# A second Strassen level for the last two products of three down stages

## The chip, the cores and the metric

The program runs on one core of one Trainium2 chip. A core has a matrix engine (TensorE, "PE" in the profile, with its weight loads shown as "PEld"), a vector engine (VectorE, "DVE"), a scalar engine (ScalarE, "ACT"), a general engine (GpSimd, "POOL") and a queue engine (SyncE, "SP") that issues all DMA transfers of this kernel in one order. Matmuls write into PSUM, eight banks of 128 x 512 fp32; everything else lives in SBUF or in DRAM.

The metric is the device time of one execution in microseconds.

## The reference, cut to what matters

```python
def _B_ref(x, w_gate, w_up, w_down):
    g = jnp.einsum("bsd,df->bsf", x, w_gate)
    u = jnp.einsum("bsd,df->bsf", x, w_up)
    h = g * u
    return jnp.einsum("bsf,fd->bsd", h, w_down)

x = A_x
x = x + _A_ref(_layernorm(x, axis=-1), A_wqkv, A_wo)
x = x + _B_ref(_layernorm(x, axis=-1), B_w_gate, B_w_up, B_w_down)
x = x + _A_ref(_layernorm(x, axis=-1), A_wqkv, A_wo)
x = x + _B_ref(_layernorm(x, axis=-1), B_w_gate, B_w_up, B_w_down)
```

S = 2048 tokens, D = 1024, F = 3584, bf16 inputs and output. `_A_ref` is a linear attention block (32 heads); `_B_ref` is the block that the change touches, in particular its last product, h times w_down. Both blocks run twice with the same weights.

## The kernel before, in words

The host code writes a list of operations per engine; `_Prog` finds every dependency from byte ranges in SBUF and from PSUM banks (a bank is one unit: whoever touches it waits for the others' last access), and turns it into semaphore waits. Each engine runs its list in order. So the order of the code is the order of every queue, SP's too.

Layer A computes K and Q (L780), a Gram matrix (L862) and the output projection (L954). Layer B works in two passes of 1024 tokens; each pass has a gate-up stage (L1037, and L1104 for products with a second level) and a down stage (L1312). The four down stages begin near 410, 654, 1132 and 1375 us of the profile: layer one's first and second pass, layer two's first and second pass.

All big products use Strassen's method in the Winograd form, seven products of half-size blocks instead of eight. In a down stage (`down`, L1278) the order is `DPROD = 1 2 7 4 6 5 3`. One product multiplies 1792 of F (14 chunks of 128, `NJ = 14`) by 512 tokens (4 tiles `t` of 128) and 512 output columns: for each tile two groups of seven matmuls, 128 x 512 each, into one bank. The stationary operand is a slice of the activations (hA, hB, hC, hD, 14 x 512 fp16 each), the moving operand is the weight block. Products 1, 2, 3 read blocks of w_down; 5, 6, 7, 4 read sums of such blocks, made in layer one's first gate-up stage (`wd_prep`) and kept in DRAM (`t_scratch`). After each tile VectorE evicts the bank (`stt`, L671: scale and add) and in products 1, 2, 7, 4 also updates a slice of the activations (`tt`, L668, 1792 elements) for later products. Product 3 accumulates onto product 5's bank, product 6 onto 1's, 4 onto 7's. Rest sums stand in `rtmp[0..7]`, 2 KB each from `O_R`.

Weights come through a ring of `NR = 5` slots of 8 KB per partition. `ring_issue` (L638) loads the unit `n` into slot (n + 1) % 5; it is called as a unit is used up, so loads run up to five units ahead. A pass has 28 gate-up units and 14 down units (two halves of 0.9 MB per product). Waiting for a free slot holds up all that follows on SP.

Some gate-up products already run a second level (`L2SETS`, `l2_of`, L1086): there a 128 x 512 result in one bank is made of seven quarter products of 256 columns, with a seed copy on ScalarE (L1119), a copy of product 5 (L1129) and a join on VectorE (L1122). Their weight sums are kept in `sp_scratch` and read by `sp_load`. The first steps of the next pass's gate-up stage (`pro`) are dealt out between the groups of product 3 of the down stage before (L1321).

Other work between the groups of a down stage: `dticks0` (first pass) takes sums of the normalised inputs off a list (`x_pop`), stores the residual (`stash`) and loads `sp_scratch`; `dticks1` (second pass, layer one) loads the K and Q weights for the next layer A (L1404 to L1407) and starts the normalisation of four token tiles. The K weights lie in the bytes of ring slots 0 and 1, the Q weights in those of hC and hD.

## Time and profile before

| | |
|---|---|
| Time, median of 3 runs | 1464.74 us (1464.23 to 1464.97) |
| Time of the profiled execution | 1464.57 us |
| Its span, first to last instruction | 1462.8 us |
| Granted TensorE clock | 1.0 of full speed |
| TensorE busy | 1453.9 us |
| VectorE, ScalarE, GpSimd busy | 1090.1, 572.0, 225.8 us |
| DMA | 298.11 MB, mean 204 GB/s |

[...] A group's row gives its line, engine, operation, shapes and count, then the busy time, the mean duration in ns, and the idle time of that engine right before these instructions with what ended it. A row of a timeline gives the start, the length, the instruction and its count, and in brackets the idle time before it. A row of windows gives the stretch, then each engine's busy time and instruction count, the granted clock, DMA's busy share and GB/s.

### The profile page before, as it was taken

To read this page: it belongs to the slowest core of one execution; us is meant where nothing else is said; L and a number is where in the kernel's file an instruction comes from. 1 tells how busy PE (TensorE), PEld (TensorE's weight loads), DVE (VectorE), ACT (ScalarE), POOL (GpSimd) and SP (SyncE) were. 2 spreads that over 40 slices of the span, in tenths; PEclk is the share of its full clock that TensorE was granted. 3 is DMA by queue.
4 is the path that set the end of the run, shared out by engine and by line. 5 is a ranking of instruction groups with operands and counts; after the bars stand their busy time and mean duration, and the time that the engine had idled before them with its cause. 6 is when DMAs were issued, how large, how long until landed. Compare 5 with 4: busy or idle time off the path is not lost.

```text
span 1462.8 us, 20720 instructions
## 1 busy us (share of the span) xinstructions
PE 1453.9 (99%) x7830; PEld 751.8 (51%) x7830; DVE 1090.1 (75%) x1990; ACT 572.0 (39%) x1178; POOL 225.8 (15%) x239
## 2 busy tenths in 40 slices
PE   8999999999999999999999999999999999999999
PEld 3444444444444555554444444456666446666544
DVE  7986888777757699865578769879877575777653
ACT  3332355333300255550023323567776005777400
POOL 4553632000000000000034337300000000000000
PEclk9999999999999999999999999999999999999999
DMA  6133667988875799975374337679986768888642
GB/s 230 37 94 107 138 131 188 278 259 259 279 253 190 259 274 291 281 242 187 127 231 123 106 108 152 152 211 272 284 258 199 243 221 240 263 264 241 217 167 94
DMA packets 370931, 298.11 MB, mean 204 GB/s; under 512 B 234640, under 2 KB 323472, under 8 KB 370832
## 3 DMA queue, kind: packets, MB, share of 16 engines
q1 hardware_dynamic: 370832, 296.80, 69.6%
q8 instruction: 61, 1.00, 0.3%
q14 instruction: 38, 0.31, 0.1%
HBM read 218.63 MB, written 54.53 MB: 187 GB/s over the span
## 4 chain that ended last, share of the span: by engine, by line
PE 99%; DMA 1%; DVE 0%; ACT 0%; SPq 0%; issue 0%
PE ps L1037 30%; PE ps L1312 23%; PE ps L780 15%; PE ps L1104 15%; PE ps L862 8%; PE ps L954 7%; DMA arena<-in_A_wqkv_dram 1%; PE ps L902 0%; PE ps L874 0%; SPq L406 0%; PE ps L538 0%; DVE arena L668 0%; ACT arena L540 0%; PE ps L886 0%; DVE arena L671 0%; DVE arena L960 0%
## 5 line engine op out<-in xcount | busy, mean ns | idle before, releaser
L671 DVE SCALAR_TENSOR_TENSOR arena<-ps,arena 128x512 f16<-128x512 f32 (+2 forms) x508 | 340.4, 686 | 195.1 <-PE ps L1312 140.8
L1037 PE MATMUL ps<-arena 128*128 128x512 f16 x2016 | 478.5, 379 | 0.0
L668 DVE TENSOR_TENSOR arena<-arena 128x512 f16<-128x512 f16 (+4 forms) x624 | 308.8, 520 | 54.1 <-ACT arena L1147 46.4
L1312 PE MATMUL ps<-arena 128*128 128x512 f16 (+1 forms) x1568 | 340.9, 379 | 0.0
L1037 PEld LDWEIGHTS ps<-arena 128*128 128x128 f16 (+1 forms) x2016 | 192.3, 98 | 186.7 <-ACT arena L1042 13.6
L1104 PE MATMUL ps<-arena 128*128 128x256 f16 x1960 | 259.4, 273 | 0.8 <-DVE ps L1122 0.5
L1312 PEld LDWEIGHTS ps<-arena 128*128 128x128 f16 x1568 | 153.4, 98 | 183.1
L1104 PEld LDWEIGHTS ps<-arena 128*128 128x128 f16 (+1 forms) x1960 | 190.9, 98 | 83.3 <-DVE ps L1122 3.8
L780 PE MATMUL ps<-arena 128*128 128x512 bf16 x1024 | 223.7, 379 | 3.2 <-ACT arena L540 1.1
L1042 ACT ACTIVATE arena<-ps 128x512 f16<-128x512 f32 x224 | 133.8, 597 | 110.6 <-PE ps L1037 108.6
L582 ACT ACTIVATE arena<-ps 128x512 f32<-128x512 f32 x128 | 76.4, 597 | 231.5 <-PE ps L780 220.1
L780 PEld LDWEIGHTS ps<-arena 128*128 128x128 f16 x1024 | 99.6, 98 | 122.0 <-DMA arena<-in_A_wqkv_dram 1.6
L1119 ACT COPY ps<-ps 128x256 f32<-128x256 f32 x168 | 61.8, 368 | 204.0 <-PE ps L1104 201.4
L435 POOL TENSOR_SCALAR arena<-arena 128x1 f32<-128x1 f32 x64 | 27.2, 425 | 643.0 <-DVE arena L434 643.0
L862 PE MATMUL ps<-arena 128*128 128x512 bf16 x512 | 115.4, 379 | 0.0
L954 PE MATMUL ps<-arena 128*128 128x512 bf16 x512 | 111.0, 379 | 0.0
L1067 ACT COPY ps<-ps 128x512 f32<-128x512 f32 x112 | 64.2, 573 | 90.6 <-PE ps L1037 52.4
L1122 DVE TENSOR_TENSOR ps<-ps,arena 128x256 f32<-128x256 f32 x168 | 70.7, 428 | 33.6 <-PE ps L1104 16.7
L432 DVE BATCH_NORM_STATS2 arena<-arena 128x6 f32<-128x512 bf16 x128 | 88.2, 689 | 8.2 <-DMA arena<-in_A_x_dram 6.0
L585 DVE SCALAR_TENSOR_TENSOR arena<-ps,arena 128x512 bf16<-128x512 f32 x128 | 88.5, 692 | 4.4
L809 POOL TENSOR_TENSOR arena<-arena 128x1024 f16<-128x1024 f32 x32 | 79.3, 2478 | 72.9 <-DVE arena L807 71.7
L792 POOL TENSOR_TENSOR arena<-arena 128x512 f32<-128x512 f32 x60 | 74.7, 1249 | 87.1 <-DVE arena L585 85.7
(51 smaller groups left out, 705.3 us busy)
## 6 DMA issues: line engine op xcount, KB each, us to landing
arena<-w_scratch SPq DMA_DIRECT2D x84, 512.0 KB, 5.4
arena<-t_scratch SPq DMA_DIRECT2D x32, 896.0 KB, 5.7
arena<-sp_scratch SPq DMA_DIRECT2D x56, 512.0 KB, 6.0
arena<-in_B_w_down_dram SPq DMA_DIRECT2D x24, 896.0 KB, 5.8
w_scratch<-arena SPq DMA_DIRECT2D x28, 512.0 KB, 6.6
sp_scratch<-arena SPq DMA_DIRECT2D x28, 512.0 KB, 4.1
arena<-in_A_wqkv_dram SPq DMA_DIRECT2D x12, 1024.0 KB, 8.0
arena<-in_B_w_gate_dram SPq DMA_DIRECT2D x42, 256.0 KB, 5.4
```

What stands on the lines that cost most here:

```text
L432: P.add("dve", (lambda h: lambda e: e.bn_stats(st[j][:, 6 * h:6 * h + 6], x_res[:, i, (D // 2) * h:(D // 2) * (h + 1)]))(h), rd=r_x(i, (D ...
L585: P.add("dve", lambda e: e.scalar_tensor_tensor(out=dst_ap, in0=psb(bank), scalar=0.0, in1=etmp[r], op0=ALU.max, op1=ALU.add), prd=[bank], ...
L668: P.add("dve", lambda e: e.tensor_tensor(out=out, in0=a, in1=b, op=op), rd=rd, wr=wr, prd=prd)
L671: P.add("dve", lambda e: e.scalar_tensor_tensor(out=out, in0=a, scalar=sc, in1=b, op0=ALU.mult, op1=op1), rd=rd, wr=wr, prd=prd)
L780: return [e.matmul(psb(bank), xnT[:, k, i * 128:(i + 1) * 128], w[:, k, h * 512:(h + 1) * 512], start=(k == 0), stop=(k == KT - 1)) for k ...
L809: P.add("pool", lambda e: e.tensor_tensor(out=asb[b].rearrange("p (h c) -> p h c", c=32), in0=pbuf.rearrange("p (h c) -> p h c", c=32), in ...
L862: return [e.matmul(psb(bank), xr[:, t, j * 128:(j + 1) * 128], pk[:, h, t, :], start=(t == 0), stop=(t == NST - 1)) for t in range(NST)]
L954: return [e.matmul(psb(bank), xnT[:, g, i * 128:(i + 1) * 128], wp[:, g, dh * 512:(dh + 1) * 512], start=(dh == 0 and g == 0), stop=(g == ...
L1037: P.add("pe", lambda e: [e.matmul(psb(bank), w[:, k, :], x[:, k, :], start=(start and k == 0), stop=(k == 3), skip_group_check=True) for k ...
L1042: P.add("act", lambda e: e.activation(t, psb(bank), AF.Copy, scale=SG), prd=[bank], wr=r)
L1104: P.add("pe", lambda e: [e.matmul(psb(bank)[:, 256 * half:256 * half + 256], w[:, k, :], xx[:, k, :], start=(start and k == 0), stop=(k == ...
L1312: return [e.matmul(psb(bank), hv[:, 7 * hf + k, t * 128:(t + 1) * 128], w[:, k, :], start=(start and hf == 0 and k == 0), stop=(hf == 1 an ...
```

## The change

In three of the four down stages (not layer one's first pass) products 5 and 3 are computed by a second Strassen level. A product is cut into quarters again: F in two halves of seven chunks, 512 tokens in two, 512 columns in two. Seven sub-products in the order 1, 5, 6, 7, 2, 3, 4, each for two halves `p` of 128 tokens, each of seven matmuls of 256 columns. Sub-product 1 goes to a bank `tmp[p]`, is copied by ScalarE into the result bank (`seed`), 5 is copied aside (`c5`), 6 and 7 accumulate on `tmp[p]` and are joined by VectorE into the result banks; 2, 3 and 4 accumulate there directly.

The activation sums (`a_sums`, four operations of 1792 elements per product) are made by VectorE during product 6 (for 5) and during product 5 (for 3). The weight sums (`b_sums`) are made once, in layer one's first down stage: load, eight subtractions, store to `d_scratch`, for product 5 and then for product 3. A down product with two levels takes four ring units (a, b, c, d; 0.92, 0.92, 0.92 and 0.46 MB) instead of two. Product 3 no longer accumulates on product 5's bank, so product 5's tiles are evicted twice (`evict5`). The next pass's prologue gets three steps inside product 3 instead of six. K weights are loaded in halves after sub-products 5 and 7 of product 3, Q weights after 7, and two instead of four normalisations are started there. In layer two the input sums are taken in products 2, 7, 4 instead of 6 and 5, and `sp_load` moves from product 6 to products 4 and 3. Places of a few buffers are exchanged (`O_DRAW`, `O_CP`, the second buffer of the sums of group "53").

```diff
-    O_DRAW = O_R + 12288
+    O_DRAW = O_R
...
-    O_CP = O_R
+    O_CP = O_R + 12288
...
+        L2D = "53"
         DPROD = ["1", "2", "7", "4", "6", "5", "3"]
+
+        def d_units(first, ps_):
+            r = []
+            for q in DPROD:
+                r += [(q, i) for i in ("abcd" if q in L2D and not (first and ps_ == 0) else "01")]
+            return r
...
+            di = L2D.index(q)
+            rs = R(V_L2 + 128 * di, 128)
+            lo, hi = slice(0, 7), slice(7, 14)
+            if hf == "a":
+                ap, rd = src(lo, slice(0, 256))
+                dma(vq(o, 1792).rearrange("p (j c) -> p j c", c=256), ap, r_slot(n, 0, 3584), KRR[sl], rd=rd)
...
+                l2d = L2D if not (first and ps_ == 0) else ""
+                SB = {"5": O_HC, "3": O_HA}
...
+                def a_sums(q):
+                    hv, ho = hs[q]
+                    blk = {(r, k): (hv[:, 7 * k:7 * k + 7, 256 * r:256 * r + 256], _seg(ho + 7168 * k, 7, 1024, 512 * r, 512 * r + 512))
+                           for r in range(2) for k in range(2)}
+                    s = [(vh(SB[q] + i * 3584, 1792).rearrange("p (j s) -> p j s", s=256), R(SB[q] + i * 3584, 3584)) for i in range(3)]
+
+                    def op(o, a, b, f):
+                        tt(o[0], a[0], b[0], f, a[1] + b[1], o[1])
+                    return [lambda: op(s[0], blk[1, 0], blk[1, 1], ALU.add),
+                            lambda: op(s[1], s[0], blk[0, 0], ALU.subtract),
+                            lambda: op(s[2], blk[0, 1], s[1], ALU.subtract),
+                            lambda: op(blk[1, 0], blk[0, 0], blk[1, 0], ALU.subtract)]
...
+                def b_load(q):
+                    for i, (_, j0, j1) in enumerate(PB):
+                        v, r = b_buf(i, vb if q in "123" else vh)
+                        src = wd_v[:, :, 1, 512:1024] if q == "3" else tscr[0]
+                        for h in range(2):
+                            dma(v[:, h], src[:, 7 * h + j0:7 * h + j1, :], R(r[0][0] + h * 1024 * (j1 - j0), 1024 * (j1 - j0)), KDB[2 * i + h],
+                                rd=[] if q == "3" else R(V_D, NJ * 32))
...
+                        res.append([lambda blk=blk: op(blk(0, 0), blk(0, 1, nf), blk(0, 0, nf)),
+                                    lambda blk=blk: op(blk(0, 1), blk(1, 1, nf), blk(0, 1, nf)),
+                                    lambda blk=blk: op(blk(1, 1), blk(1, 1, nf), blk(0, 0)),
+                                    lambda blk=blk: op(blk(1, 0), blk(1, 0, nf), blk(1, 1))])
+                    return [(lambda f=f, g=g: [f(), g()]) for f, g in zip(*res)]
...
+                def prep_step(q, t):
+                    k = 4 * "1274".index(q) + t
+                    if k == 0:
+                        b_load("5")
+                        EX.extend(b_sums("5") + [lambda: b_store("5"), lambda: b_load("3")] + b_sums("3") + [lambda: b_store("3")])
+                    if k in (3, 4, 5, 6, 8, 12, 13, 14, 15):
+                        ex_pop(2 if k == 8 else 1)
+                    if k == 15:
+                        ex_pop(9)
...
+                def evict5(t, bank):
+                    pb = psb(bank)
+                    xs, rx = xq(1, 1, t)
+                    stt(xs, pb, CD, rtmp[t], rr(t), rx, prd=[bank])
+                    final(1, 1, t)
+                    stt(rtmp[4 + t], pb, CD, rtmp[4 + t], rr(4 + t), rr(4 + t), prd=[bank])
+
+                def evict3(t, bank):
+                    xs, rx = xq(0, 1, t)
+                    stt(xs, psb(bank), CD, rtmp[4 + t], rr(4 + t), rx, prd=[bank])
+                    final(0, 1, t)
...
+                    dst, tmp = ([6, 7, 5, 4], [0, 2]) if q == "5" else ([0, 1, 2, 3], [6, 7])
...
+                    def seed(p, b):
+                        P.add("act", lambda e: e.copy(psb(b)[:, 0:256], psb(tmp[p])[:, 0:256]), prd=[tmp[p]], pwr=[b])
+
+                    def join(p, b):
+                        P.add("dve", lambda e: e.tensor_tensor(out=psb(b)[:, 256:512], in0=psb(tmp[p])[:, 0:256], in1=c5[p][0], op=ALU.add),
+                              prd=[tmp[p]], rd=c5[p][1], pwr=[b])
+
+                    for si, i in enumerate((1, 5, 6, 7, 2, 3, 4)):
+                        for p in range(2):
+                            hi, lo = dst[p], dst[p + 2]
+                            if i == 1:
+                                mm(1, p, tmp[p], 0, True)
+                                seed(p, hi)
+                            elif i == 5:
+                                mm(5, p, tmp[p], 1, False)
+                                P.add("act", (lambda p: lambda e: e.copy(c5[p][0], psb(tmp[p])[:, 256:512]))(p), prd=[tmp[p]], wr=c5[p][1])
+                            elif i == 6:
+                                mm(6, p, tmp[p], 0, False)
+                                join(p, hi)
+                            elif i == 2:
+                                mm(2, p, hi, 0, False)
+                            elif i == 3:
+                                mm(3, p, hi, 1, False)
+                                evict(p, hi)
+                            elif i == 7:
+                                mm(7, p, tmp[p], 0, False)
+                                seed(p, lo)
+                                join(p, lo)
+                            else:
+                                mm(4, p, lo, 0, False)
+                                evict(p + 2, lo)
+                            if q == "3" and i in (3, 4) and (i == 4 or p):
+                                pro_step(pro, 1)
+                        if q == "5" and i in (1, 7):
+                            ex_pop(2)
+                        if i in (5, 7, 3, 4):
+                            ring_issue()
+                            ticks(q, {5: 0, 7: 1, 3: 2, 4: 3}[i])
...
                 for qi, q in enumerate(DPROD):
+                    if q in l2d:
+                        if q == "5":
+                            ex_pop(4)
+                            EX.extend(a_sums("3"))
+                        two_level(q)
+                        continue
+                    if q == "6" and l2d:
+                        EX.extend(a_sums("5"))
...
+                        if q in "1274" and first and ps_ == 0:
+                            prep_step(q, t)
+                        if q == "6" and l2d and t < 2:
+                            ex_pop(2)
...
-                if q == "6" and t == 3 and not first:
-                    for g in SPG:
-                        sp_load(1, 0, g)
-                    sp_load(1, 1, "12")
-                if q in "65":
-                    x_pop(2 if q == "6" else 3)
+                if q == "4" and t < 2 and not first:
+                    sp_load(1, t, "12")
+                    if t == 0:
+                        sp_load(1, 0, "53")
+                if q in ("65" if first else "274"):
+                    x_pop(3 if q == "5" else 1 if q == "2" else 2)
...
+                if q == "3" and t == 0 and not first:
+                    sp_load(1, 1, "53")
...
-                if q == "5" and t == 3:
-                    for w in "kq":
-                        load_w(w, 0)
-                        load_w(w, 1)
+                if q == "3" and t < 2:
+                    load_w("k", t)
+                if q == "3" and t == 1:
+                    load_w("q", 0)
+                    load_w("q", 1)
                 if q == "3":
                     stash(12 + t)
-                    nxt.step_t(1)
-                    nxt.b2_one()
-                    nxt.b1_one()
-                    nxt.start(8 + t)
+                    for k in ((0,) if t == 1 else (1,) if t == 2 else ()):
+                        nxt.step_t(1)
+                        nxt.b2_one()
+                        nxt.b1_one()
+                        nxt.start(8 + k)
```

More of the change, by code (lines that the diff above doesn't have):

```diff
@@ L270, in build_kernel @@
     V_SP = V_D + NJ * 32
[L271 removed]
+    V_L2 = V_SP + NJ * 64
+    P = _Prog(V_L2 + 256)
     dma_keys = []
@@ L294, in build_kernel @@
     KTL = [dkey("tl%d" % i) for i in range(4)]
+    KDB = [dkey("db%d" % i) for i in range(4)]
+    KDS = [dkey("ds%d" % i) for i in range(4)]
     KTF = [dkey("tf%d" % i) for i in range(NST)]
@@ new lines, in down, with ex_pop @@
+                EX = []
+                def ex_pop(n=1):
+                    for _ in range(n):
+                        if EX:
+                            EX.pop(0)()
+                def evict5(t, bank):
[8 more added lines that the diff above has]
+                    final(0, 1, t)
```

115 lines of the change are left out of this document (90 added, 25 removed).

## The prediction

> **What bounds the kernel now.** I read the page first (span, busy shares, chain of waits), then the groups with shapes kept apart, then the timeline of the down stages.
>
> ```profile
> span 1462.8 us, 20720 instructions
> PE 1453.9 (99%) x7830; PEld 751.8 (51%) x7830; DVE 1090.1 (75%) x1990; ACT 572.0 (39%) x1178; POOL 225.8 (15%) x239
> PE 99%; DMA 1%; DVE 0%; ACT 0%; SPq 0%; issue 0%
> ...
> L1312 PE MATMUL ps<-arena 128*128 128x512 f16 x896 | 194.0, 379 | 0.0
> L1312 PE MATMUL ps<-arena 128*128 128x512 bf16 x672 | 148.1, 379 | 0.0
> L1104 PE MATMUL ps<-arena 128*128 128x256 f16 x1960 | 259.4, 273 | 0.8 <-DVE ps L1122 0.5 <-ACT arena L1147 0.2
> ```
>
> TensorE is busy from end to end and the chain is TensorE. The down matmuls (L1312) have 0.0 us of idle before them; even the two-level products of gate-up (L1104), with their copies and adds on other engines, lose 0.8 us in 1960. So the change is worth the TensorE time it removes, less every wait it brings into a queue that today has almost none.
>
> The mean durations (379, 273 ns) overlap; the price of a matmul is its pitch, read from long runs:
>
> ```profile
> 412.15 75.70 PE L1312 MATMUL ps<-arena 128*128 128x512 bf16 x350
> ...
> 1227.20 2.35 PE L1104 MATMUL ps<-arena 128*128 128x256 f16 x20
> ```
>
> 512 columns: (75.70 - 0.379) / 349 = 0.2158 us. 256 columns: (2.35 - 0.273) / 19 = 0.1093 us, though each has its own weight load.
>
> **Term 1, TensorE work.** A down product is 4 tiles x 14 = 56 matmuls of 512 columns: 56 x 0.2158 = 12.09 us. A two-level product is 7 groups x 2 halves x 7 = 98 matmuls of 256 columns: 98 x 0.1093 = 10.71 us. Two products in three stages: 6 x 1.375 = **-8.25 us**. It cannot gain more.
>
> On the loads, row first:
>
> ```profile
> L1312 PEld LDWEIGHTS ps<-arena 128*128 128x128 f16 x1568 | 153.4, 98 | 183.1
> ```
>
> A load takes 98 ns, so it hides under 109 ns with 11 to spare, as it does in the run of 20. [...]
>
> **Term 2, waits inside a two-level product.** A group of seven lasts 0.764 us; the two halves alternate, so each hand-over to ACT or DVE has one group as cover. The rows:
>
> ```profile
> 489.64 0.38 PE L1104 MATMUL ps<-arena 128*128 128x256 f16 x2
> 490.06 0.43 DVE L1122 TENSOR_TENSOR ps<-ps,arena 128x256 f32<-128x256 f32 x1 [1.52 <-PE ps L1104]
> ...
> 974.53 0.43 DVE L1122 TENSOR_TENSOR ps<-ps,arena 128x256 f32<-128x256 f32 x1 [0.88 <-ACT ps L1119]
> 975.02 0.33 PEld L1104 LDWEIGHTS ps<-arena 128*128 128x128 bf16 x4 [0.32 <-DVE ps L1122]
> ...
> L1119 ACT COPY ps<-ps 128x256 f32<-128x256 f32 x168 | 61.8, 368 | 204.0 <-PE ps L1104 201.4
> L1129 ACT COPY arena<-ps 128x256 f32<-128x256 f32 x84 | 32.0, 381 | 0.0
> ```
>
> A consumer starts 0.31 us after the last matmul's start (489.75 to 490.06); TensorE goes on 0.06 us after the releaser's end (974.96 to 975.02). From a group's start, its last matmul starts at 0.65, the consumer at 0.96, and TensorE is free again at 0.96 + 0.37 + 0.06 = 1.39 (seed copy), 1.40 (copy of c5), 1.45 (join, 0.43). The next group on that bank is due at 1.53. All three fit, by 80 to 140 ns, if ACT and DVE are free. ACT has nothing else in a down stage. DVE has:
>
> ```profile
> 708.06 1.08 DVE L668 TENSOR_TENSOR arena<-arena 128x1792 f16<-128x1792 f16 x1
> 710.48 2.01 DVE L671 SCALAR_TENSOR_TENSOR arena<-ps,arena 128x512 bf16<-128x512 f32 x3 [1.33 <-PE ps L1312]
> 713.50 2.01 DVE L671 SCALAR_TENSOR_TENSOR arena<-ps,arena 128x512 bf16<-128x512 f32 x3 [1.01 <-PE ps L1312]
> ```
>
> Product 6 takes three evictions per tile of 3.02 us, 1.01 us idle. The change adds four sums of 1792 elements (1.08 each, about 1.0 apart) in its first two tiles. DVE falls behind and is level again by the last tile, whose evictions end 2.1 us into product 5. There two dependent sums for product 3 (a_sums) stand ahead of the first join: to 4.3 us. The join is ready at 5 x 0.764 + 0.2 = 4.0, ends at 4.75, and TensorE wants the bank at 4.58: 0.24 us late. Product 5's tiles now take two evictions each (evict5), behind two more sums; the second tile's bank comes free about 11.8 us after product 5's start, and product 3 wants it at 11.7: 0.13 us. So 0.4 us per stage, **+1.1 us** for three. Bounds: 0 (below that is excluded, no wait exists to be removed), and 6 us if one more 2.01 us eviction group stands before the joins in each stage.
>
> **Term 3, next pass's prologue.** In layer two's first down stage these steps lie between product 3's groups of seven:
>
> ```profile
> 1209.11 0.60 PE L1104 MATMUL ps<-arena 128*128 128x256 f16 x4
> 1209.55 1.67 PE L1312 MATMUL ps<-arena 128*128 128x512 bf16 x7
> 1211.06 0.38 PE L1104 MATMUL ps<-arena 128*128 128x256 f16 x2
> 1211.27 1.67 PE L1312 MATMUL ps<-arena 128*128 128x512 bf16 x7
> ```
>
> Six steps have 1.51 us of cover each. After the change three steps have 0.76 us and the others follow back to back. Step 16 waits for two copies (0.31 + 0.37 + 0.38 against 0.76 + 0.11), 17 for a join behind an eviction, 21 for 17's join, 36 for 31's copies behind a 0.57 us copy: 0.14 + 0.17 + 0.2 + 0.3 = **+0.8 us**, once (layer one's first stage is not converted). Bounds 0 and 2.
>
> **Term 4, preparation in the first down stage.** Two loads and two stores of 14 x 128 KB = 1.83 MB, and eight pairs of subtractions of 1536 and 256 elements. On the line through 512 elements (0.42) and 1792 (1.08) a pair costs 1.25 us, 10 us in all.
>
> ```profile
> 410.00:422.00 12.00, 12.00 (x57) 5.48 (x56) 8.28 (x14) 0.00 (x0) 0.00 (x0) 1.00 0.92 322
> 422.00:434.00 12.00, 12.00 (x58) 5.44 (x56) 6.76 (x8) 0.00 (x0) 0.00 (x0) 1.00 0.45 153
> ...
> 445.58 1.83 SPq L406 DMA_DIRECT2D arena<-t_scratch  x2
> ...
> t_scratch<-arena SPq DMA_DIRECT2D x1, 512.0 KB, 3.7
> ```
>
> DVE has 5 of 12 us free, DMA half. The adds have cover: product 2's banks are wanted again only by product 7, 12 us later. What can surface is the order. The first load queues behind five x loads and lands near 426.5; the sum at product 1's last tile wants it at 423, so DVE runs 4 us late, under that cover. SP then holds the second load until the first stores have landed (about 440 to 451), and the two weight loads issued today at 445.58 to 447.41 stand behind it. The first of the two carries the second half of product 6's weights, wanted at 459.9; I get 459.5. Finally T1's subtraction in product 6 waits for the second store. Three places with 0 to 3 us of slack: **+0.7 us**, bounds 0 and 5.
>
> **Term 5, K weights of layer two.** Moved from product 5's end to inside product 3, because they overlay ring slots 0 and 1; the Q loads follow them on SP, and two normalisation starts move into layer A.
>
> ```profile
> 730.11 5.22 SPq L406 DMA_DIRECT2D arena<-in_A_wqkv_dram  x4
> DMA to landing us min/median/max: 5.1/5.1/5.1
> DMA to landing us min/median/max: 7.7/7.7/7.7
> ...
> 743.51 103.76 PE L780 MATMUL ps<-arena 128*128 128x512 bf16 x480
> 764.00:774.00 10.00, 10.00 (x48) 4.56 (x47) 9.25 (x17) 3.58 (x6) 4.00 (x5) 1.00 0.35 98
> ```
>
> Today they are issued 13 us ahead; the first half lands in 5.1 us, the second 2.6 behind it. Now half 0 goes out 3.2 us into product 3 and lands at 8.4 of its 10.8; half 1 at 6.3, landing about 11.5, wanted after one group of eight (1.73 us), at 12.4. **+0.2 us**, bounds 0 and 2.6. The moved normalisations find DVE at 9.25 of 10 us, but tokens are needed four groups later; 0.
>
> **Term 6, weight supply.** Products 5 and 3 read 0.92 + 0.92 + 0.92 + 0.46 = 3.2 MB each instead of 1.83, partly in 512 B runs.
>
> ```profile
> 672.00:684.00 12.00, 12.00 (x58) 5.44 (x56) 6.67 (x9) 0.00 (x0) 0.00 (x0) 1.00 0.44 147
> 1220.00:1240.00 20.00, 20.00 (x142) 13.69 (x141) 15.28 (x31) 14.35 (x36) 0.00 (x0) 1.00 0.93 276
> ```
>
> Full DMA is 147 / 0.44 = 334 GB/s with today's 1 KB rows, 276 / 0.93 = 297 with gate-up's mixture. Need at the worst (late product 6 to the end of 3) is 0.46 + 3 x 0.92 + 0.46 for the products, 0.5 for sums and 4 x 0.9 for the next pass's units, 7.8 MB in 23 us; at 300 GB/s that takes 26. The lag of 3 us meets a lead of about 10 us (five slots ahead): **0**, bounds 0 and 15.
>
> **Sum.** Profiled execution 1464.57 (span 1462.8 and 1.8 around it; the median of the runs is 1464.74): 1464.57 - 8.25 + 1.1 + 0.8 + 0.7 + 0.2 + 0 = **1459.1 us**.
>
> **Rivals.**
> - *Preparation surfaces* (term 4 at its upper bound: a weight unit or DVE late behind SP's blocked queue): 1459.1 - 0.7 + 5 = 1463.4, no change. For it: slack of only 0.4 us by my count. Against: five slots, and DVE slack of about 9 us.
> - *K weights late* (term 5 at 2.6): 1461.5 to 1462, at the edge of no change. For: half the former lead; against: DMA is otherwise empty there.
> - *The hand-overs do not fit.* Place: join before group 7 and seeds before group 5. If DVE is one eviction group (2.01 us) further behind in products 5 and 3, all of it shows: 6 x 2.0 = 12, for term 2's 1.1: 1470.0, slower. It decides from 1.375 us of wait per product. For it: margins of 80 to 140 ns and sums queued ahead of joins; against: L1104 loses 0.8 us over 168 joins, though with other work between.
> - *Weights late.* If the DMA lag grows to 15 us less the 10 of lead in each stage, 3 x 5: 1474, slower. For: 3.2 MB per 10.7 us is 300 GB/s, DMA's full rate; against: only for 23 us.
> - *Loads show.* If loads stop hiding under 109 ns, 98 more matmuls' worth of 98 ns: 6 x 98 x 0.098 = 58 more, 1517. The run of 20 speaks against it.
>
> **Chances.** Forecast 0.70; K weights 0.04; preparation 0.10; hand-overs 0.08; weights late 0.06; loads 0.02. A measurement of this kernel tells 0.2% (2.9 us) from no change: faster (below 1461.8) 0.70, within 0.14, slower 0.16. Range: from no wait at all (1464.57 - 8.25 = 1456.3) to beyond preparation's case, 1465.0; it leaves out the three slower cases and a little of the others. The forecast's own range is 1456.3 to 1461.7.
>
> **What would show it.** 1232 matmuls of 512 columns left in the down loop, 588 new ones of 256 at a pitch near 109 ns; each converted stage 2.3 to 2.8 us shorter; idle TensorE before the two-level line about 1 us in all, released by DVE; idle before L780 in layer two near 0. Wrong if the pitch is above 123 ns (12.09 / 98), if TensorE's idle behind DMA is over 3 us, or if the first down stage is more than 3 us longer.

## The result and the profile after

| | before | after |
|---|---|---|
| Median of 7 runs each | 1464.74 us (1464.23 to 1465.23) | 1459.52 us (1458.97 to 1460.23) |
| Profiled execution | 1464.57 us | 1459.30 us |
| Its span | 1462.8 us | 1457.6 us |

The ratio is 0.9965 (95% interval 0.9953 to 0.9977): 5.2 us faster, 0.4 above the forecast. Line numbers have moved: the plain down matmul L1312 is now L1516, the new two-level matmul L1452 with its seed L1456, join L1459 and c5 copy L1470; gate-up's second level L1104 is L1143, its join L1161 and copies L1168 and L1186; the K and Q projection L780 is L819; `tt` is L707, `stt` L710, every DMA issue L411.

The page of the kernel after, the row of busy shares and that of its chain of waits:

```profile
PE 1448.2 (99%) x8082; PEld 775.5 (53%) x8082; DVE 1135.5 (78%) x2066; ACT 584.8 (40%) x1214; POOL 224.8 (15%) x239
PE 96%; DVE 2%; DMA 1%; ACT 0%; SPq 0%; issue 0%
```

TensorE still sets the end, but no longer alone. At the new waits the chain passes over to the engine that is waited for: DVE and DMA hold 3% of it instead of 1%. The groups of the same kernel, shapes kept apart:

```profile
L1516 PE MATMUL ps<-arena 128*128 128x512 f16 x728 | 157.8, 379 | 0.0
L1516 PE MATMUL ps<-arena 128*128 128x512 bf16 x504 | 110.6, 379 | 0.0
L1452 PE MATMUL ps<-arena 128*128 128x256 f16 x462 | 52.6, 273 | 0.1
L1452 PE MATMUL ps<-arena 128*128 128x256 bf16 x126 | 15.1, 273 | 0.0
L1143 PE MATMUL ps<-arena 128*128 128x256 f16 x1960 | 259.3, 273 | 1.2 <-DVE ps L1161 0.5 <-ACT arena L1186 0.3 <-DMA arena<-in_B_w_gate_dram 0.3
```

728 + 504 = 1232 matmuls of 512 columns are left, 462 + 126 = 588 of 256 columns are new. The idle time of L1452 reads 0.1 us, which is too little: a matmul's recorded duration (273 ns) is longer than the pitch (109 ns), so a start that is 0.15 us late still overlaps the matmul before it. Short waits are therefore read from the starts of neighbouring matmuls, beyond the pitch. TensorE's timeline around layer one's converted stage:

```profile
719.22 21.86 PE L1452 MATMUL ps<-arena 128*128 128x256 f16 x196
740.91 1.89 PE L819 MATMUL ps<-arena 128*128 128x512 bf16 x8
743.64 36.65 PE L819 MATMUL ps<-arena 128*128 128x512 bf16 x169 [0.84 <-DMA arena<-in_A_wqkv_dram]
```

Products 5 and 3 take 740.91 - 719.22 = 21.69 us, where two plain ones take 2 x 12.09 = 24.17 by the prediction's pitch: 2.48 us less. 196 x 0.1093 is 21.42, so 0.27 us of waits lie inside the pair. The last two rows show the one large new wait: eight matmuls of the K projection, then 743.64 - 740.91 = 2.73 us to the ninth, of which eight pitches of 0.2158 explain 1.73. The remaining 1.0 us is waiting for the second half of the K weights.

The weight loads of the next pass's prologue, inside layer two's first down stage, from the timeline of PEld (a prologue step waits here for what the bracket names):

```profile
1211.51 0.33 PEld L1143 LDWEIGHTS ps<-arena 128*128 128x128 bf16 x4 [0.53 <-DMA arena<-in_B_w_gate_dram]
...
1212.86 0.11 PEld L1143 LDWEIGHTS ps<-arena 128*128 128x128 f16 x2 [0.25 <-ACT arena L1168]
...
1214.01 0.99 PEld L1143 LDWEIGHTS ps<-arena 128*128 128x128 f16 x10 [0.27 <-DVE ps L1161]
1215.31 0.33 PEld L1143 LDWEIGHTS ps<-arena 128*128 128x128 bf16 x4 [0.32 <-DVE ps L1161]
1216.08 1.21 PEld L1143 LDWEIGHTS ps<-arena 128*128 128x128 f16 x12 [0.43 <-ACT arena L1186]
```

The brackets are the loader's idle time, of which some 0.1 us is ordinary. From the starts of neighbouring matmuls the five waits of TensorE are 0.42, 0.14, 0.16, 0.21 and 0.31 us. Four were predicted with their places; the first was not. Where it comes from is seen in SP's timelines of the kernel after and of the kernel before, at the same load:

```profile
1203.25 1.53 SPq L411 DMA_DIRECT2D out_dram<-arena  x2
1204.82 0.43 SPq L411 DMA_DIRECT2D arena<-in_B_w_gate_dram  x1
```

```profile
1192.68 0.39 SPq L406 DMA_DIRECT2D arena<-in_B_w_gate_dram  x1
```

In the kernel after, the gate weights stand on SP behind two output stores, which wait for the last evictions of product 5. Issued at 1204.82, they were used at 1211.51, 6.7 us later. In the kernel before, the same load went out at 1192.68 for a step that began at 1209.11, 16.4 us ahead. So most of the lead was lost elsewhere: a two-level product takes four units of the five-slot ring instead of two, and a load that runs five units ahead now goes out when product 5's last unit is used up, not product 6's.

The sum, all from starts of matmuls in this one execution: 8.25 us of work gone; waits inside the three pairs of products +0.89 (0.27, 0.35, 0.27); prologue +1.23, and +0.1 on a DMA 21 us later; K weights +1.0; preparation 0. That makes -5.0; the spans differ by 5.2.

### The profile page after: what moved, and what is told of

Its sections match the earlier page's. It is cut to its first block, busy times and chain, and to the rows that moved or that the text cites. A ratio compares the mean times of both kernels' runs of the same rounds, so it can differ in the third digit from the quotient of the medians.

```text
span 1457.6 us, 21384 instructions
## 1 busy us (share of the span) xinstructions
PE 1448.2 (99%) x8082; PEld 775.5 (53%) x8082; DVE 1135.5 (78%) x2066; ACT 584.8 (40%) x1214; POOL 224.8 (15%) x239
## 4 chain that ended last, share of the span: by engine, by line
PE 96%; DVE 2%; DMA 1%; ACT 0%; SPq 0%; issue 0%
PE ps L1076 30%; PE ps L1516 17%; PE ps L819 15%; PE ps L1143 15%; PE ps L901 8%; PE ps L993 7%; PE ps L1452 3%; DMA arena<-in_A_wqkv_dram 1%; DVE arena L710 1%; DVE arena L707 1%; PE ps L913 0%; PE ps L941 0%; DMA arena<-in_B_w_gate_dram 0%; SPq L411 0%; PE ps L543 0%; ACT arena L1186 0%
## 5 line engine op out<-in xcount | busy, mean ns | idle before, releaser
L710 DVE SCALAR_TENSOR_TENSOR arena<-ps,arena 128x512 f16<-128x512 f32 (+2 forms) x520 | 346.1, 686 | 125.4 <-PE ps L1516 66.7
L707 DVE TENSOR_TENSOR arena<-arena 128x512 f16<-128x512 f16 (+6 forms) x664 | 342.7, 543 | 66.6 <-ACT arena L1186 47.6
L1516 PE MATMUL ps<-arena 128*128 128x512 f16 (+1 forms) x1232 | 267.5, 379 | 0.0
L1143 PE MATMUL ps<-arena 128*128 128x256 f16 x1960 | 259.3, 273 | 1.2 <-DVE ps L1161 0.5
L1143 PEld LDWEIGHTS ps<-arena 128*128 128x128 f16 (+1 forms) x1960 | 190.6, 98 | 83.7 <-DVE ps L1161 4.4
L819 PE MATMUL ps<-arena 128*128 128x512 bf16 x1024 | 223.8, 379 | 3.5 <-DMA arena<-in_A_wqkv_dram 1.6
L1516 PEld LDWEIGHTS ps<-arena 128*128 128x128 f16 x1232 | 120.5, 98 | 144.5
L819 PEld LDWEIGHTS ps<-arena 128*128 128x128 f16 x1024 | 99.5, 98 | 122.5 <-DMA arena<-in_A_wqkv_dram 2.6
L1158 ACT COPY ps<-ps 128x256 f32<-128x256 f32 x168 | 61.9, 368 | 128.0 <-PE ps L1143 125.4
L1456 ACT COPY ps<-ps 128x256 f32<-128x256 f32 x24 | 8.6, 357 | 218.3 <-PE ps L1452 156.1
L1161 DVE TENSOR_TENSOR ps<-ps,arena 128x256 f32<-128x256 f32 x168 | 70.7, 428 | 29.6 <-PE ps L1143 13.8
```

The lines of the kernel that those rows point to most:

```text
L707: P.add("dve", lambda e: e.tensor_tensor(out=out, in0=a, in1=b, op=op), rd=rd, wr=wr, prd=prd)
L710: P.add("dve", lambda e: e.scalar_tensor_tensor(out=out, in0=a, scalar=sc, in1=b, op0=ALU.mult, op1=op1), rd=rd, wr=wr, prd=prd)
L819: return [e.matmul(psb(bank), xnT[:, k, i * 128:(i + 1) * 128], w[:, k, :], start=(k == 0), stop=(k == KT - 1)) for k in range(KT)]
L1143: P.add("pe", lambda e: [e.matmul(psb(bank)[:, 256 * half:256 * half + 256], w[:, k, :], xx[:, k, :], start=(start and k == 0), stop=(k == ...
L1516: return [e.matmul(psb(bank), hv[:, 7 * hf + k, t * 128:(t + 1) * 128], w[:, k, :], start=(start and hf == 0 and k == 0), stop=(hf == 1 an ...
```

## The experiments

Each edit is made to the kernel after, and none leaves out a part of the computation. The moment at which the first down stage begins differs between executions by up to 1.6 us, although nothing ahead of it is edited. TensorE's timelines of the kernel after and of e8_banks, at that place:

```profile
409.66 1.67 PE L1516 MATMUL ps<-arena 128*128 128x512 bf16 x7
...
412.03 75.70 PE L1516 MATMUL ps<-arena 128*128 128x512 bf16 x350
```

```profile
413.59 75.70 PE L1516 MATMUL ps<-arena 128*128 128x512 bf16 x347
```

The long run begins 1.56 us later in e8 (the records of 3 of its 350 matmuls are missing). So for single runs the table gives, beside the time, the rest: the span of the profiled execution less the start of its first down stage, which lies 2.37 us (412.03 - 409.66) ahead of this long run.

| run | time, us | runs | rest, us |
|---|---|---|---|
| before | 1464.74 | 7 | 1053.1 |
| after | 1459.52 | 7 | 1047.9 |
| e1_prep_only | 1465.16 | 10 | 1053.2 |
| e2_last_only | 1462.53 | 10 | 1050.7 |
| e3_k_swap | 1458.43 | 1 | 1046.8 |
| e4_q_late | 1459.78 | 1 | 1048.4 |
| e5_sums_3_1 | 1462.11 | 1 | 1050.7 |
| e6_sums_1_1_2 | 1459.18 | 1 | 1046.9 |
| e7_ring_first | 1458.14 | 1 | 1046.4 |
| e8_banks | 1460.96 | 1 | 1048.0 |
| e9_dma_plus1 | 1461.08 | 1 | 1049.4 |
| e10_dma_plus2 | 1475.48 | 1 | 1063.3 |
| e11_best_nobanks | 1457.48 | 4 | 1045.8 |
| e12_best | 1458.74 | 5 | 1046.9 |

**What the preparation and the moves cost.** e1 keeps both but runs every product plain:

```diff
-                r += [(q, i) for i in ("abcd" if q in L2D and not (first and ps_ == 0) else "01")]
+                r += [(q, i) for i in "01"]
...
-                l2d = L2D if not (first and ps_ == 0) else ""
+                l2d = ""
```

> The weight sums are made and stored, and every move of the change stays, but no down product runs the second level. My theory (the gain is TensorE's 1.375 us per product; preparation and the moved loads are hidden under it): 1464.7 us, within 0.5 of the kernel before, first down stage 86.6 us long as before. Rival (preparation costs something and the second level gains more than 8.25 us): slower than before by 0.7 to 5 us, with idle TensorE in the first down stage.

Measured: 1465.16 us against 1464.77 for the kernel before beside it, ratio 1.0003 (0.9993 to 1.0012). Preparation, the moved loads and the moved sums together are not told from nothing; by the interval they cost at most 1.8 us. In the profiles they cost nothing where the sums are made: from its first to its last matmul start the first down stage lasts 86.56 us before, after and in e1, and its 350 matmuls in a row take the same 75.70 us before and after. The one place where they could show is VectorE's timeline in the kernel after:

```profile
424.26 0.96 DVE L707 TENSOR_TENSOR arena<-arena 128x1536 f16<-128x1536 f16 x1 [2.78 <-DMA arena<-t_scratch]
426.53 0.29 DVE L707 TENSOR_TENSOR arena<-arena 128x256 f16<-128x256 f16 x1 [1.31 <-DMA arena<-t_scratch]
...
453.00 0.96 DVE L707 TENSOR_TENSOR arena<-arena 128x1536 f16<-128x1536 bf16 x1 [4.33 <-DMA arena<-in_B_w_down_dram]
456.59 0.29 DVE L707 TENSOR_TENSOR arena<-arena 128x256 f16<-128x256 bf16 x1 [2.63 <-DMA arena<-in_B_w_down_dram]
```

VectorE did stand idle for its loads, 4.1 and 7.0 us in all, and TensorE did not wait for it.

**Where the gain lies.** e2 runs the second level in layer two's second pass alone.

```diff
-                l2d = L2D if not (first and ps_ == 0) else ""
+                l2d = L2D if not first and ps_ == 1 else ""
...
-            return ps_ * (NU + len(d_units(first, 0)))
+            return ps_ * (NU + 14)
```

> Only layer two's second down stage runs the second level. My theory: the gain is local and per product: 2 x 1.375 - 0.27 of waits = 2.5 us, 1462.2 us, and the last down stage is 82.0 us from first to last matmul start where it was 84.4 before; no idle at the K weights of layer two or in the prologue of its second pass. Rival (the gain comes from what the other moves do): last stage shorter by 2.5 us but the total outside 1461.5 to 1463.

Measured: 1462.53 us, ratio 0.9984 (0.9975 to 0.9994), 2.2 us below the kernel before beside it. TensorE's timeline of e2:

```profile
1436.48 21.86 PE L1452 MATMUL ps<-arena 128*128 128x256 f16 x196
```

It is the same 21.86 us as in layer one of the kernel after. So the gain is local, some 2.4 us a stage, and the waits inside a pair don't hang on whether the other stages are converted. The waits behind a stage do belong to its conversion: e2, with those two stages plain, has neither the K wait nor the new prologue waits.

**The K weights.** e3 lets layer two's attention use the first halves for two tokens before any second half is wanted:

```diff
+            if not first:
+                for h in range(2):
+                    for i in range(NHOLD):
+                        proj_k(tok[i], h)
+                seq = seq[NHOLD:]
             for kind, i in seq:
```

> In layer two's attention block the first two token tiles run both their first halves of K before their second halves, so the second half of the K weights is wanted 1.73 us later; nothing else changes. My theory (only that half is late, by 1.0 us): TensorE's idle before the K projections falls from 1.0 to 0 us, about 1458.5. Rival (the whole boundary is late, whoever is first): idle stays near 1 us.

TensorE's timeline of e3 where the projection begins:

```profile
741.12 7.07 PE L819 MATMUL ps<-arena 128*128 128x512 bf16 x32
```

The wait is gone. The second half, issued at 736.73, took 7.2 us here too and landed at 743.9: too late for the old order, which wanted it at 742.85 (eight pitches after 741.12), and in time for the new one at 744.57. So the order removed the wait, not a faster load: the second half of K was wanted one group too early. Time and rest are 1.1 us lower. That the sum fits is partly chance, for two waits that the edit does not touch changed as well: the gate weights 0.04 instead of 0.42 us, a DMA at 1236 0.29 instead of 0.10 us. Why is that half late? One theory was that the Q weights, issued right behind it, take its share of the DMA engines. e4 issues them after product 3:

```diff
                 if q == "3" and t < 2:
                     load_w("k", t)
-                if q == "3" and t == 1:
-                    load_w("q", 0)
-                    load_w("q", 1)
...
                     if t == 3:
+                        load_w("q", 0)
+                        load_w("q", 1)
                         for k in range(4):
                             stash(8 + k)
```

> The two Q loads are issued after product 3's last sub-product instead of right behind the second K load. Theory A (the Q loads share the DMA engines with the K half that they follow and stretch its 7.1 us): it lands in 5.1 to 5.6 us, idle falls from 1.0 to 0 us. Theory B (transfers are served in the order of issue and the half is late only because it goes out late): it still takes about 7 us and idle stays at 1.0 us; the Q weights come 4 us later, still in time.

The time from issue to landing of the second half of K, and the window from its issue to its landing (the last two columns are the DMA engines' busy share and GB/s; the share counts packets whole by their start, so it can pass 1), first of the kernel after, then of e4:

```profile
DMA to landing us min/median/max: 7.1/7.1/7.1
...
736.50:743.60 7.10, 6.30 (x50) 4.64 (x48) 6.09 (x13) 0.95 (x2) 1.58 (x4) 1.00 1.08 369
```

```profile
DMA to landing us min/median/max: 7.3/7.3/7.3
...
736.50:743.80 7.30, 6.34 (x51) 4.67 (x48) 6.29 (x13) 0.95 (x2) 1.58 (x4) 1.00 1.06 376
```

The half is 1 MB. It takes 7.1 us, all the while with full DMA engines, and 7.3 us with Q moved. But the edit moved Q by much less than meant, as SP's timelines show, again of the kernel after and then of e4:

```profile
736.52 3.17 SPq L411 DMA_DIRECT2D arena<-in_A_wqkv_dram  x3
```

```profile
738.58 2.85 SPq L411 DMA_DIRECT2D arena<-in_A_wqkv_dram  x2
```

SP runs ahead of TensorE, which reached the K projection at 740.95, so Q went out at 738.58 instead of 736.93, only 1.7 us later, while the K half was on its way until 743.8; and three residual stores moved up into Q's old place (376 GB/s). So e4 decides neither theory: what slows the half stays open. The wait also varies. With the K part unchanged it was 1.0 (after), 1.4 (e5), 1.1 (e6), 0 (e7), 1.2 (e8) and 0.9 us (e9), all read from starts. The half landed in 7.1 us (after), 7.2 (e3) and 7.3 (e4); in e7 it went out at 736.91 and nothing waited for it at 743.24 (eight pitches after 741.51), so it took at most 6.3. Why is open too.

**The hand-overs inside a two-level product.** The prediction said that two sums ahead of the first join make it 0.24 us late. e5 puts three there, e6 one:

```diff
                         if q == "5" and i in (1, 7):
-                            ex_pop(2)
+                            ex_pop(3 if i == 1 else 1)
```

```diff
-                        if q == "5" and i in (1, 7):
-                            ex_pop(2)
+                        if q == "5" and i in (1, 6, 7):
+                            ex_pop(2 if i == 7 else 1)
```

> The same work, but three instead of two of product 3's activation sums stand on VectorE ahead of product 5's first join (and one instead of two behind the last). My theory (a join late behind VectorE's queue shows in full on TensorE): the wait before sub-product 7 grows from 0.15 to 0.23 us by about 1.0 us in each of three stages, stages 1.0 us longer, 1462.3 us. Rival (hand-overs have hidden cover, a later join costs little): stages within 0.3 us of the changed kernel, 1459 to 1460.

> The same work, one sum ahead of the first join, one right behind the two joins, two as before. My theory: the wait before sub-product 7 falls from 0.15 to 0.23 us to under 0.02 in each stage, the other wait (0.12 at product 3's second half) stays, 1458.8 us. Rival (these waits are the chain of hand-overs itself, not VectorE's queue): they stay.

VectorE and then TensorE in the kernel after, in e5 and in e6:

```profile
721.35 2.21 DVE L707 TENSOR_TENSOR arena<-arena 128x1792 f16<-128x1792 f16 x2
723.48 0.96 DVE L1459 TENSOR_TENSOR ps<-ps,arena 128x256 f32<-128x256 f32 x2
```

```profile
721.35 3.33 DVE L707 TENSOR_TENSOR arena<-arena 128x1792 f16<-128x1792 f16 x3
...
725.08 16.98 PE L1452 MATMUL ps<-arena 128*128 128x256 f16 x154 [1.12 <-DVE ps L1459]
```

```profile
721.92 1.08 DVE L707 TENSOR_TENSOR arena<-arena 128x1792 f16<-128x1792 f16 x1
723.81 0.43 DVE L1459 TENSOR_TENSOR ps<-ps,arena 128x256 f32<-128x256 f32 x1 [0.81 <-PE ps L1452]
...
719.79 21.69 PE L1452 MATMUL ps<-arena 128*128 128x256 f16 x196
```

With two sums the join begins as soon as VectorE is free, at 723.48; with three it is 1.1 us later, and TensorE waits 1.28 us in place of 0.15. With one, VectorE itself waits 0.81 us for the matmuls and TensorE's 196 take 21.69 us in place of 21.86. A sum of 1.08 us ahead of the join is paid in full at that wait: the cover was used up already. The pair in e5 is 1.0 us longer, for the 0.12 us at product 3's second half is gone there. e6's rest is 1.0 us lower than that of after; the three join waits explain 0.54 of it, and the 0.4 us wait on the gate weights did not occur either.

The other wait, 0.12 us at product 3's second half, was put down to bank 7, which product 5's second eviction frees late. e8 gives product 3 other banks:

```diff
-                    dst, tmp = ([6, 7, 5, 4], [0, 2]) if q == "5" else ([0, 1, 2, 3], [6, 7])
+                    dst, tmp = ([6, 7, 5, 4], [0, 2]) if q == "5" else ([0, 2, 7, 6], [1, 3])
```

> Product 3 makes its first sub-products in banks 1 and 3, free since product 4, instead of 6 and 7, which product 5's evictions read; its results go to 0, 2, 7, 6. My theory (product 3's second half waits for the eviction of bank 7): the three waits of 0.12 us go, converted stages 0.12 us shorter; the steps of the prologue that use banks 6 and 7 may wait up to 0.3 us more, once. Rival (the wait has another cause, such as the weights): 0.12 us stays.

TensorE's timeline of e8, a converted pair:

```profile
720.78 21.72 PE L1452 MATMUL ps<-arena 128*128 128x256 f16 x196
```

The pair is 0.14 us shorter, and the 0.12 us wait is gone in all three pairs, so the bank was the cause. The prologue's waits grew from 1.23 to 1.53 us. Most of that, 0.23 us, is the wait for the gate weights (0.65 instead of 0.42), which the edit does not touch; the steps that wait for the evictions of product 3, which now end on banks that the prologue wants, lost 0.07 us. The rest is 0.1 us higher than that of after, for the K wait was 0.2 us longer too. The time of 1460.96 alone would mislead: this execution began its first down stage 1.6 us late.

**The order on SP.** e7 issues the next weights ahead of product 5's last two evictions and their stores:

```diff
+                            elif q == "5":
+                                mm(4, p, lo, 0, False)
+                                if p:
+                                    ring_issue()
+                                    evict(2, dst[2])
+                                    evict(3, dst[3])
...
                         if i in (5, 7, 3, 4):
-                            ring_issue()
+                            if q != "5" or i != 4:
+                                ring_issue()
```

> In product 5 the ring load that follows sub-product 4 is put on the DMA queue ahead of the output stores of the last two tiles, which wait for VectorE's evictions. My theory (the prologue's first step waits 0.4 us for gate weights whose issue stood behind those stores): the gate weights of layer two's second pass go out at least 1 us earlier and the 0.4 us wait goes, 1458.9 us. Rival (the wait is the DMA engines' backlog, 6 to 7 us to landing): they land at the same time, wait 0.3 to 0.5 us as before.

SP's and TensorE's timelines of e7:

```profile
1202.30 0.66 SPq L411 DMA_DIRECT2D arena<-in_B_w_gate_dram  x1
...
1204.61 1.68 SPq L411 DMA_DIRECT2D out_dram<-arena  x2
...
1210.47 0.60 PE L1143 MATMUL ps<-arena 128*128 128x256 f16 x4
```

The gate weights go out ahead of the stores, 8.2 us before their use instead of 6.7, and the 0.4 us wait is gone. The rest is 1.5 us lower, more than this edit can explain: in this execution the K wait of 1.0 us did not occur either, though nothing of it was changed. And the gate wait is not constant where the order is as in the kernel after: 0.42 (after), 0.04 (e3), 0.39 (e4), 0.65 (e8), 0 in e5 and e6. Those loads landed in 6.6, 6.3, 6.6, 6.8, 5.1 and 5.2 us. So the shown cause is a margin near zero, which the landing time decides from run to run; the edit adds about 2 us of margin.

**The weight supply.** e9 and e10 copy 0.92 MB from DRAM to DRAM, into a buffer that nobody reads, with unit b of each two-level product (e10: with b and c):

```diff
+    jscr = nc.dram_tensor("j_scratch", (12, 128, NJ, 256), F16, kind="Internal").ap()
...
+            if hf in "b":
+                dma(jscr[jn[0]], dscr[di][:, :, 256:512], [], KOUT, rd=rs)
+                jn[0] += 1
```

> With each unit b of a two-level product a further 0.92 MB is copied from one DRAM buffer to another that nothing reads, on the same DMA queue; nothing waits for it but the end. A product now asks for 4.1 MB in 10.7 us, 390 GB/s. My theory (a lead of about 10 us covers a few us of backlog in the stage; what has less lead pays): no wait for weights inside products 5 and 3; the K half of layer two and the prologue's gate weights each 2 to 4 us later; total 1462 to 1468 us. Rival (DMA is already at the edge in the stage): waits on DMA inside products 5 and 3 in all three stages, over 5 us, 1468 us or more.

> The same with units b and c: 5.0 MB per product, 470 GB/s asked for, about 6 us more per product than the engines can move. My theory: now the lead is used up, waits on weights appear inside product 3, and the gate weights and K weights are late by 8 us or more: 1472 to 1490 us. Rival (the DRAM to DRAM copies do not compete): as with one copy.

Windows around layer two's converted products, first of the kernel after and then of e10 (the same columns):

```profile
1180.00:1215.00 35.00, 34.68 (x263) 25.06 (x261) 28.49 (x45) 5.47 (x16) 0.00 (x0) 1.00 0.83 246
1420.00:1456.00 36.00, 34.73 (x257) 24.65 (x255) 28.44 (x42) 4.34 (x12) 0.00 (x0) 1.00 0.64 193
```

```profile
1180.00:1215.00 35.00, 33.90 (x232) 22.28 (x230) 29.75 (x47) 4.35 (x12) 0.00 (x0) 1.00 0.96 288
1420.00:1456.00 36.00, 36.00 (x229) 22.03 (x227) 28.85 (x40) 3.26 (x9) 0.00 (x0) 1.00 0.81 245
```

e9 loses 1.5 us of rest, most of it in two waits for weights inside product 3 (0.79 and 0.55 us): the lead still covers nearly all of one extra copy a product. What was expected of e9 failed in its places: no wait was expected inside the products, and the K half, expected 2 to 4 us later, cost a wait of 0.9 us where it was 1.0 before. e10 loses 15.4. So the supply of the kernel after is covered, at a DMA share of 0.83 and 0.64, and the cover ends at about one more copy. Of e10's 15.4 us the waits explain only some 9: TensorE was also slower after the longer ones. Its timeline in e10:

```profile
738.58 4.76 PE L1457 MATMUL ps<-arena 128*128 128x256 bf16 x42 [1.27 <-DMA arena<-in_B_w_down_dram]
...
1216.07 4.90 PE L1457 MATMUL ps<-arena 128*128 128x256 bf16 x28 [2.10 <-DMA arena<-in_B_w_down_dram]
...
1463.31 7.60 PE L1457 MATMUL ps<-arena 128*128 128x256 bf16 x42 [2.97 <-DMA arena<-in_B_w_down_dram]
```

The pitch is (4.76 - 0.273) / 41 = 0.109 us after the wait of 1.27, but (4.90 - 0.273) / 27 = 0.171 and (7.60 - 0.273) / 41 = 0.179 after the longer two. The windows of e10 behind the wait for the second half of K (2.8 us, it ended at 747.68) and behind the last wait, with the granted clock in the third column from the end:

```profile
749.60:752.60 3.00, 3.00 (x9) 1.01 (x7) 1.12 (x2) 0.60 (x1) 0.61 (x1) 0.54 1.08 374
```

```profile
1463.00:1467.00 4.00, 3.69 (x18) 2.64 (x19) 0.00 (x0) 0.00 (x0) 0.00 (x0) 0.50 0.26 86
```

**All together.** e11 joins e3, e6 and e7, and gives product 3 a fourth prologue step; e12 adds e8's banks.

```diff
-                            if q == "3" and i in (3, 4) and (i == 4 or p):
+                            if q == "3" and i in (3, 4):
```

> Four repairs together: K halves in the other order, one sum ahead of the first join, ring load ahead of the output stores, and four instead of three prologue steps between the last groups of product 3. My theory: waits fall by 1.0 + 0.54 + 0.4 + about 0.2 from the changed kernel, 1457.4 us. If the waits only move elsewhere: 1458.5 to 1459.5.

> The same with product 3's first sub-products in banks 1 and 3: three waits of 0.12 us less and up to 0.3 us more in the prologue, 1457.2 us, at best 0.4 below the run without the banks.

e11: 1457.48 us (1457.21 to 1457.90), ratio to the kernel before 0.9949 (0.9935 to 0.9963). Its slowest run is below the fastest of the kernel after, 1458.97, though the two were run at different times; the kernel before read 1464.94 and 1464.74 beside them. e12: 1458.74 us, ratio 0.9957 (0.9943 to 0.9971), 1.3 us slower than e11, and a miss of what was expected. TensorE's timelines of e11 and of e12 after products 5 and 3:

```profile
719.90 21.69 PE L1457 MATMUL ps<-arena 128*128 128x256 f16 x196
741.43 6.85 PE L819 MATMUL ps<-arena 128*128 128x512 bf16 x31
```

```profile
719.78 21.56 PE L1457 MATMUL ps<-arena 128*128 128x256 f16 x196
741.18 1.89 PE L819 MATMUL ps<-arena 128*128 128x512 bf16 x8
743.32 4.92 PE L819 MATMUL ps<-arena 128*128 128x512 bf16 x22 [0.25 <-DVE arena L710]
...
1214.68 1.05 PE L1148 MATMUL ps<-arena 128*128 128x256 f16 x8 [0.72 <-DVE arena L710]
```

e12's pair is the shortest of all, 0.13 us below e11's. It gives that back twice: the K projection and the prologue want banks 6 and 7, which product 3's evictions (L710) now free last, 0.42 and 0.88 us late by the starts. e8, with the same banks and without the other repairs, lost only 0.07 us of this kind in the prologue, and at the K projection it waited for the weights anyway. In e11 what is left is the three bank waits of 0.12 us and 0.83 us in the prologue.

## Why the prediction was right

The direction, the place and the mechanism held, and the time is 0.4 us off. By its own terms:

- **Term 1, TensorE work, -8.25: right.** 588 matmuls of 256 columns run at 0.109 us. The row of 196 settles the question of the loads: with 196 loads of 128 x 128 at 98 ns, 19.2 us in all, the 196 matmuls still take 21.69 us; from 719.2 to 740.9 the loader is busy for 18.95 of the 21.70 us and the matmuls for all of them.
- **Term 2, waits inside the products, +1.1: measured +0.89.** Both places were named, and e5, e6 and e8 show the causes. Sizes: join 0.15, 0.23, 0.15 where 0.24 was predicted for each; bank 7 0.12 where 0.13 was. The first figure had the join end 4.75 us into the product; in layer one it ended at 4.69 (723.48 + 0.43 - 719.22), for VectorE began it 0.08 us before the second sum's recorded end.
- **Term 3, prologue, +0.8: measured +1.3.** The four predicted waits (0.14, 0.17, 0.2, 0.3) came as 0.14, 0.16, 0.21, 0.31. What failed is the step that looked only at engines: the gate weights of the first prologue step lost some 8 us of their lead to the ring and 2 to output stores ahead of them on SP that wait for evictions, 0.4 us, and another 0.1 us of DMA wait came at 1237. Both are inside the stated bound of 2. The size of the first changes between executions.
- **Term 4, preparation, +0.7: measured 0** (e1). VectorE was 4.1 us late at the first load, as predicted, and 7.0 at the second; the cover of 12 us held both. The 0.7 stood for places with little slack, and none of them showed.
- **Term 5, K weights, +0.2: measured +1.0,** 0 to 1.4 between executions. The issue times were as predicted (half 0 at 733.5, half 1 at 736.5, some 3 and 6 us into product 3). The step that failed is "landing about 11.5": it carried today's 5.1 us of a first half, ahead of which the engines moved 8 GB/s (728 to 730 in the kernel before), over to a half that is issued 3 us behind the first, with 2 MB of Q behind it, and takes 7.1 us. The rival's sentence that DMA is otherwise empty there doesn't fit the window: the engines were full (busy share 1.08) and moved 369 GB/s x 7.1 us = 2.6 MB, of which the half is 1. e3 shows that the wait hangs on how early the second half is wanted. What slows its landing stays open after e4, Q included, and so does why it differs between executions.
- **Term 6, supply, 0: right for the products,** and e9 and e10 show how near the bound lies. The lead of ten us was said to meet a lag of three; one extra copy a product costs 1.5 us, two cost 15. For the prologue's first load the lead was 6.7 us and not ten, which term 3 paid.

The errors have opposite signs: terms 2 and 4 were 0.9 too high, terms 3 and 5 1.3 too low, which leaves 0.4. So the forecast's closeness is in part luck; each term stayed inside its bounds.

Of the rivals, "preparation surfaces" falls by e1 (0.4 us, at most 1.8 by the interval, where it needed 5). "K weights late" has the right mechanism at two fifths of its price. "The hand-overs do not fit" would need 1.375 us of wait per product; there were 0.15 per product, and e5 shows that the mechanism is real: one more sum ahead of the join costs 1.1 us a stage. "Weights late" didn't happen, and e10 is what it looks like. "Loads show" falls by the row of 196.

## What to carry to other kernels

When a stage on TensorE's path gets shorter, price the removed matmuls by their pitch and then go through each hand-over with start, duration and due time to a tenth of a microsecond; that arithmetic came out within 0.1 us a place here. Do the same for SP's queue: for each load ask what stands ahead of it and what that waits for, and give a load issued behind another a landing time measured behind another, not the one of a load with nothing ahead of it (for a half of K 7.7 us in the kernel before and 7.1 in the kernel after, against 5.1 here). When a change uses up more slots of a ring, count each load's lead again in microseconds. Try a repair in its surroundings: beside the other repairs, the new banks removed one wait and made two larger ones where the next stage wanted the same banks.

## What the runs showed of the hardware that was not expected

**After waits of 2.3 to 3.1 us TensorE was slower.** e10 has three idle stretches of over 2 us (between starts, beyond a pitch). After those of 2.3 and 3.1 us the matmuls of 256 columns came at a mean pitch of 0.171 us (28 of them) and 0.179 us (42) instead of 0.109; behind the second the granted clock was 0.50 in the window 1463 to 1467. After the one of 2.8 us the K projection's matmuls of 512 columns came at 0.250 us in the mean (50 of them in 12.65 us) instead of 0.2158, with a granted clock of 0.84 from 747.6 to 749.6 and of 0.54 from 749.6 to 752.6. After 1.4 us they did not slow down (0.109), nor after the K waits of 0.9, 1.0 and 1.2 us in e9, in the kernel after and in e8 (0.217, 0.216 and 0.215 us a matmul). Beyond the usual pitch that is 1.7, 2.8 and 1.7 us, about 6 on top of e10's 9 of waits: the wait of 3.1 us cost 6.0 in all.

**The landing time of an unchanged load varies by more than these margins.** The first gate load, issued at the same place of the order, landed in 5.1 to 6.8 us, so a wait behind it was 0 in two executions and 0.65 us in another. The second half of K took 7.1 us in the kernel after and at most 6.3 in e7, where nothing of it was edited, and its wait was 0 to 1.4 us over the runs. A margin smaller than such a spread, 1.7 us for the gate load and 1.4 us of wait for the K half, is a chance and not a cover.
